# Key and value products in two parts, statistics ordered apart, and another hand-written order: a fused linear-attention and feed-forward kernel

## The chip, the cores and the metric

The kernel runs on one core of a Trainium2 chip. The metric is the device time of one execution in microseconds (us). Before the change it is 236.49 us, the median of three runs (236.43 to 236.63).

A core has five engines that run their own instruction streams and meet through semaphores: TensorE (PE in the profile, with its weight loads listed as PEld), VectorE (DVE), ScalarE (ACT), GpSimd (POOL) and SyncE (SP), which here only starts transfers. PSUM has eight banks, into which TensorE writes its products; everything else works from SBUF.

## The reference

The input is one sequence of 2048 tokens with 640 features, in bfloat16. There are 32 heads of 20 features, and a hidden layer of 1728.

```python
qkv = x_norm @ wqkv                       # x_norm: layer norm of x, without scale
pq = einsum("bhsd,hdf->bhsf", q, w_phi)   # 20x20 feature map per head; pk alike
phi_q = concat([softmax(pq), softmax(-pq)])       # phi_k alike
kv  = einsum("bhsf,bhsd->bhfd", phi_k, v)
z   = einsum("bhsf->bhf", phi_k)
o   = einsum("bhqf,bhfd->bhqd", phi_q, kv) / (phi_q . z + 1e-6)
h   = x + o @ wo
out = h + silu(layernorm(h) @ w1) @ w2
```

The attention has no mask and no product of queries with keys: all keys and values are first summed into one 40x20 matrix per head, which every query then uses.

## The kernel before

The tokens are cut into 16 tiles of 128. The feature dimension of 640 is five chunks of 128. The work of a tile is a set of small steps, each a Python function `op_xx(t)`; their names appear below as in the code.

- Layer norm 1: `st` takes the statistics of tile t (two instructions over 320 features each and one that aggregates, VectorE, lines 273 and 274); `rs` makes the reciprocal root of the variance and the bias (a power and small steps on POOL, lines 280 to 289; one small step on VectorE for a single tile, line 278); `xn` normalises (VectorE, line 297, or ScalarE, line 302, by the suffix v or a). The tile is then transposed, either on TensorE with a copy out of PSUM (`xt`, line 308, and `xc`) or by a transposing DMA (`xd`).
- Weights: the key weights are transposed on TensorE (`wt`, line 322, with the copy `wc`) and multiplied by the block-diagonal feature map (`fk`, line 337; copied to SBUF by `fc`), so that one product gives the mapped keys. The feature map's block-diagonal form is made by `mk` (a mask) and `ph` (the product of mask and map, VectorE, line 198). The query weights come by transposing DMA (`lq`) and are folded by `gk` and `gc`. Copies out of PSUM are lines 169 (VectorE) and 171 (ScalarE).
- Keys and values: `kp` is the key product of a tile and `vp` its value product, ten matmuls of 320 columns each (line 370, function `proj`: five chunks, two halves). `vc` copies the values to one of ten buffers `Vp`, whose last column is one, filled by `mo` (line 207). `ke` takes the two exponentials (ScalarE, line 395), `kr` their sums per head and the reciprocals (VectorE, lines 403 and 406), `kn` multiplies the keys by them: wholly on POOL (suffix p), wholly on VectorE (v), or three quarters (q) or one quarter (d) on POOL and the rest on VectorE (lines 414 and 418). `cc` adds the tile's keys and values into the matrices of all heads: 32 small matmuls (line 427).
- Queries: `qp`, `qs`, `qr`, `qt` are the parts of a query product (line 457) for a group of tiles, `qe` the exponentials (ScalarE, line 479). Groups of tiles are 0-1, 2-5, 6-9, 10-13, 14-15.
- Attention of a tile: `dp` is 40 small matmuls (line 504), `dw`, `dr` and `do` form the quotient on VectorE and POOL (lines 522 to 539), `td` a transposing DMA.
- Output product `op` (line 566), residual sum `oa` (VectorE, line 575), sum of squares `sq` (ScalarE, line 583), layer-norm factors `sr` (POOL, lines 588 to 598), normalisation `hn` (VectorE, line 605, or POOL and ScalarE, lines 610 and 613), transposing DMA `hd`.
- Feed-forward: `up` (lines 645 and 655) and its activation `ua` for a group and a piece of the hidden layer, `yp` and `yh` (lines 691 and 704) per tile and half, `yo` and `yz` the last sum and the store.
- Loads: `lx` (x), `lk`, `lp`, `lv`, `lo`, `l1`, `l2`, `lh` on SyncE's or ScalarE's queue; warm-up matmuls `wm` (line 268).

All orders are written by hand. The string `ORDER` holds one word per step: name, arguments, engine or split, and after `@` the PSUM banks. The loop at the end of the kernel calls the functions in that order under a manual schedule, so each engine executes its instructions in exactly the order in which the words stand; only semaphores between the engines are added. No planner or cost model moves anything afterwards. A word that stands early can hold up everything behind it on its engine if its input is late.

In the order before, the ten fills `mo` stand second; the first weight transposes are followed by the first folding products; the mask product stands right behind the first tile's statistics; the key-value sums come in five runs with tiles 9 1 0 11, then 4 5 2 3 12, 8 13 10, 6 7, and 15 14.

Of the kernel before, what the change touches and what calls it, by code (L numbers as in the profile page):

```python
# [30 lines left out]
lx.12.16.s vp.1@6 st.10 xt.2@5 vp.0@0 xc.2.a xn.9.a vc.0.a vp.2@2 st.11 lo.2.5.s xn.3.v xt.3@4 xc.3.a  # L31
rs.10.12 xn.8.a vc.2.a vc.1.a kp.2@0 ke.2 st.4 xd.9 st.5 kp.3@4 lo.0.2.s ke.3 rs.4.6 vp.3@2 xn.11.v vp.9@6
vc.9.a xn.4.a kp.9@0 ke.9 vc.3.a st.12 st.13 st.6 rs.12.14 xd.8 kr.1 kn.1.p kp.8@4 ke.8 mc.1 xn.13.a xn.12.a
xd.11 vp.11@6 vp.8@0 vc.8.a xn.5.v kr.0 kp.11@2 lq.2.s ke.11 st.7 rs.6.8 xn.6.a st.14 st.15 rs.14.16 xd.4
kr.9 vp.4@4 vc.4.a xd.5 vp.5@0 kn.0.p vc.11.a kr.2 vc.5.a kn.9.p kp.5@2 kr.11 kn.11.p gk.2@4 xn.10.a gc.2.a
xd.12 vp.12@6 vc.12.v kr.3 kn.3.p kp.4@0 xn.15.a ke.4 kp.12@4 cc.9 cc.1 kr.4 kn.4.p cc.0 xn.14.v cc.11 ke.5
kr.5 kn.2.d xd.13 ke.12 kr.12 lq.4.s xd.6 kp.6@0 lq.0.s ke.6 vp.13@2 vc.13.a kp.13@4 ke.13 vp.6@0 xd.15
xd.10 gk.4@2 vp.10@4 vc.6.a lq.3.s gk.3@0 gc.4.a gc.3.a vc.10.a kn.5.q kp.10@2 kn.12.p kr.6 xn.7.a l1.3.s
kn.6.q lq.1.s gk.1@0 gc.1.a kr.13 kn.13.p cc.4 cc.5 l1.0.s ke.10 kr.10 cc.2 cc.3 cc.12 xd.14 xd.7 kr.8
kn.8.p kn.10.d vp.15@4 vc.15.a kp.15@0 ke.15 kp.14@2 gk.0@4 gc.0.a vp.7@0 ke.14 kr.14 kn.14.p qp.0.1@4  # L40
qs.0.1 qr.0.1 kp.7@2 ke.7 l2.10.13.s kr.15 l1.2.s cc.8 vc.7.v cc.13 l2.2.4.s cc.10 qt.0.1 qp.0.0@2 qs.0.0
kn.15.p qr.0.0 qt.0.0 qe.0.1 l2.4.6.s kr.7 kn.7.v l2.6.8.s qe.0.0 vp.14@0 vc.14.a qp.0.2@6 qs.0.2 cc.6 cc.7
mt qe.0.2 cc.15 cc.14 kc km.0 lh.s qp.3.0@4 qs.3.0 qr.3.0 km.1 dp.0@0 l1.4.s close dw.0.p dr.0 qt.3.0
do.0.1.p qe.3.0 qp.2.0@6 qs.2.0 qr.2.0 qt.2.0 qe.2.0 do.0.0.p dp.1@0 dw.1.p qp.1.0@4 dr.1 do.1.0.p qs.1.0
qr.1.0 qt.1.0 qe.1.0 qp.1.1@6 td.0 do.1.1.p td.1 dp.3@0 dw.3.p dr.3 do.3.0.p qs.1.1 qr.1.1 qt.1.1 qe.1.1
qp.3.2@4 qp.1.2@5 dp.2@0 dw.2.p qs.1.2 qe.1.2 do.3.1.p td.3 qs.3.2 op.0@6 dr.2 do.2.1.p do.2.0.p qe.3.2 oa.0
dp.4@0 dw.4.p td.2 sq.0 qp.2.2@5 qs.2.2 qe.2.2 op.1@6 oa.1 sr.0 qp.2.1@4 dp.6@0 dw.6.p l1.5.s l1.1.s qs.2.1
qr.2.1 hn.0.a hd.0 sq.1 qt.2.1 sr.1 hn.1.v hd.1 qe.2.1 op.3@6 oa.3 sq.3 dp.5@0 dw.5.p op.2@4 sr.3 oa.2
hn.3.a sq.2 dr.5 do.5.0.p do.5.1.p qp.3.1@6 qs.3.1 l2.0.2.s l2.8.10.s qr.3.1 dp.9@0 dw.9.p td.5 dr.9
do.9.0.p dr.6 do.6.1.p dr.4 do.4.1.p do.4.0.p td.4 qt.3.1 qe.3.1 up.0.2@4 ua.0.2 dp.7@0 sr.2 up.0.0@6 ua.0.0  # L50
dw.7.p dr.7 up.0.3@4 ua.0.3 do.6.0.p dp.8@0 dw.8.p dr.8 hn.2.a up.0.1@6 ua.0.1 td.6 do.8.0.p op.5@4 oa.5
dp.12@0 dw.12.p dr.12 yp.1.0@6 do.7.1.p do.7.0.p sq.5 td.7 hd.3 op.4@4 oa.4 sr.5 hn.5.v hd.5 do.9.1.p sq.4
td.9 sr.4 hn.4.a dp.10@0 dw.10.p yp.1.1 yp.0.1@4 yh.0.0 hd.2 hd.4 yo.1 dp.11@0 dw.11.p dr.11 do.8.1.p
do.11.0.p td.8 yp.0.0 yo.0 op.7@6 oa.7 sq.7 dr.10 op.6@0 oa.6 sq.6 sr.6 op.9@2 up.1.6@4 do.11.1.v td.11 oa.9
sq.9 dp.15@0 ua.1.6 sr.9 up.1.5@6 ua.1.5 up.1.1@4 hn.9.v hd.9 do.10.0.p dw.15.p dr.15 hn.6.v hd.6 op.8@6
oa.8 sq.8 op.11@0 ua.1.1 sr.7 hn.7.v hd.7 up.1.3@2 oa.11 do.12.1.p sr.8 hn.8.v do.15.0.p dp.14@4 dw.14.p
dr.14 do.14.0.v hd.8 ua.1.3 up.1.4@0 ua.1.4 do.14.1.v td.14 up.1.0@2 sq.11 sr.11 hn.11.v ua.1.0 up.2.6@4
ua.2.6 dp.13@0 dw.13.p dr.13 do.13.1.p up.2.0@6 up.2.5@4 ua.2.5 op.14@0 up.1.2@2 ua.2.0 oa.14 sq.14 up.2.2@4
ua.1.2 do.12.0.p td.12 sr.14 op.12@6 oa.12 ua.2.2 hn.14.v do.10.1.p do.15.1.v yp.4.0@0 up.2.4@2 ua.2.4 td.10
op.10@4 oa.10 up.2.1@6 sq.12 sr.12 hn.12.a hd.11 hd.12 up.2.3@2 ua.2.1 yp.2.0@4 ua.2.3 yp.9.0@6 do.13.0.p  # L60
# [697 lines left out]
```

## Time and profile before

| what | value |
|---|---|
| median of three runs | 236.49 us |
| profiled execution, own time | 236.35 us |
| its span | 234.4 us |
| TensorE busy | 230.5 us, 98% of the span, 2674 matmuls |
| TensorE weight loads | 148.4 us, beside the matmuls |
| VectorE busy | 133.5 us, 249 instructions |
| ScalarE busy | 114.5 us, 171 instructions |
| POOL busy | 95.4 us, 190 instructions |
| granted TensorE clock | 1.00 in all stages |

The span is the time from the first to the last instruction in the trace; the execution is some 2 us longer, for what lies around it. Busy time is a sum over stages. The engines beside TensorE are close to full only in the first part: between 38 and 68 us VectorE is busy 28.19 of 30 us, between 160 us and the end 13.89 of 74.4.

How to read it: a row of the chain gives start, length and the work that ended last; a row of the timeline gives start, length, engine, line, output and input with their shapes, and in square brackets how long the engine had been idle and for what it waited; a row of a group gives busy time and the mean length in nanoseconds of one instruction. Consecutive chain pieces of TensorE hide short waits inside them; they show when equal pieces have unequal lengths.

### The profile page before, as it was taken

To read this page: it belongs to the slowest core of one execution; us is meant where nothing else is said; L and a number is where in the kernel's file an instruction comes from. 1 tells how busy PE (TensorE), PEld (TensorE's weight loads), DVE (VectorE), ACT (ScalarE), POOL (GpSimd) and SP (SyncE) were. 2 spreads that over 40 slices of the span, in tenths; PEclk is the share of its full clock that TensorE was granted. 3 is DMA by queue.
4 is the path that set the end of the run, shared out by engine and by line. 5 is a ranking of instruction groups with operands and counts; after the bars stand their busy time and mean duration, and the time that the engine had idled before them with its cause. 6 is when DMAs were issued, how large, how long until landed. Compare 5 with 4: busy or idle time off the path is not lost.

```text
span 234.4 us, 6307 instructions
## 1 busy us (share of the span) xinstructions
PE 230.5 (98%) x2674; PEld 148.4 (63%) x2674; DVE 133.5 (57%) x249; ACT 114.5 (49%) x171; POOL 95.4 (41%) x190
## 2 busy tenths in 40 slices
PE   8999999999999999999999999999999999999995
PEld 4777777776554556876645455556776865566662
DVE  3999999999968899788956641301341310001132
ACT  3789996885857776742244536260040015613000
POOL 7485798997904455765285123141040000000000
PEclk9999999999999999999999999999999999999999
DMA  7967758839101375325823202123212300000112
GB/s 203 381 234 147 82 112 110 182 64 350 37 3 31 59 176 148 59 49 98 142 55 61 56 3 55 30 57 63 88 24 57 106 27 5 0 3 2 54 34 81
DMA packets 44844, 20.67 MB, mean 88 GB/s; under 512 B 34448, under 2 KB 44304, under 8 KB 44816
## 3 DMA queue, kind: packets, MB, share of 16 engines
q1 hardware_dynamic: 43728, 19.88, 36.1%
q10 hardware_dynamic: 1088, 0.39, 0.8%
q8 instruction: 21, 0.34, 0.6%
q14 instruction: 7, 0.06, 0.1%
HBM read 9.61 MB, written 2.62 MB: 52 GB/s over the span
## 4 chain that ended last, share of the span: by engine, by line
PE 98%; ACT 1%; DVE 0%; issue 0%
PE mm L691 24%; PE mm L645 24%; PE mm L370 19%; PE mm L457 10%; PE mm L566 9%; PE mm L504 3%; PE mm L268 2%; PE mm L427 2%; PE mm L337 1%; PE mm L655 1%; PE mm L704 1%; ACT EqT L479 1%; PE mm L322 1%; PE mm L308 0%; DVE ob L721 0%
## 5 line engine op out<-in xcount | busy, mean ns | idle before, releaser
L691 PE MATMUL mm<-w,shT 128*128 128x320 bf16 (+2 forms) x416 | 58.7, 299 | 0.0
L645 PE MATMUL mm<-HnT,w 128*128 128x512 bf16 (+1 forms) x325 | 58.6, 337 | 0.0
L691 PEld LDWEIGHTS <-shT 128*128 128x128 bf16 x416 | 39.6, 98 | 17.2 <-issue 1.1
L667 ACT ACTIVATE shT<-mm 128x1024 bf16<-128x1024 f32 (+2 forms) x29 | 27.6, 963 | 44.6 <-PE mm L645 43.1
L712 DVE TENSOR_TENSOR ob<-mm,X 128x640 bf16<-128x640 f32 x15 | 12.3, 819 | 62.3 <-PE mm L691 59.3
L645 PEld LDWEIGHTS <-w 128*128 128x128 bf16 x325 | 31.4, 98 | 23.2
L370 PEld LDWEIGHTS <-XnT 128*128 128x128 bf16 x320 | 30.8, 98 | 12.0
L414 POOL TENSOR_TENSOR Ek<-Ek,Sk 128x1280 bf16<-128x1280 bf16 (+2 forms) x15 | 32.9, 2217 | 4.0 <-DVE Sk L406 4.0
L539 POOL TENSOR_TENSOR o<-u,rd 128x320 bf16<-128x320 f32 x28 | 19.9, 727 | 22.9 <-DVE rd L533 16.4
L583 ACT ACTIVATE sq<-X 128x640 bf16<-128x640 bf16 x16 | 11.7, 732 | 28.3 <-DVE X L575 27.2
L566 PE MATMUL mm<-wo,ot 128*128 128x320 bf16 x160 | 23.9, 299 | 0.3 <-ACT EqT L479 0.3
L457 PE MATMUL mm<-XnT,Wfq 128*128 128x512 bf16 x100 | 23.8, 380 | 0.0
L370 PE MATMUL mm<-wv,XnT 128*128 128x320 bf16 x160 | 23.7, 299 | 0.0
L370 PE MATMUL mm<-Wfk,XnT 128*128 128x320 bf16 x160 | 23.5, 299 | 0.0
L395 ACT ACTIVATE Ek<-mm 128x640 bf16<-128x640 f32 x32 | 20.5, 714 | 6.0 <-PE mm L370 5.1
L403 DVE TENSOR_REDUCE Sk<-Ek 128x64 f32<-128x1280 bf16 x16 | 23.2, 1452 | 0.3 <-ACT Ek L395 0.3
L479 ACT ACTIVATE EqT<-mm 128x1024 bf16<-128x1024 f32 (+1 forms) x24 | 19.7, 879 | 4.9 <-PE mm L457 4.8
L575 DVE SCALAR_TENSOR_TENSOR X<-mm,X 128x640 bf16<-128x640 f32 x16 | 13.0, 818 | 15.4 <-PE mm L566 15.1
L566 PEld LDWEIGHTS <-ot 128*128 128x128 bf16 x160 | 15.7, 98 | 7.3 <-issue 0.2
L273 DVE BATCH_NORM_STATS2 stats<-X 128x6 f32<-128x320 bf16 x32 | 13.6, 467 | 3.8 <-DMA X<-in_A_x_dram 3.8
L457 PEld LDWEIGHTS <-Wfq 128*128 128x128 bf16 x100 | 9.1, 98 | 9.3
L525 DVE TENSOR_TENSOR u<-mm,w 128x672 f32<-128x672 f32 x16 | 13.7, 857 | 1.2 <-DVE w L523 0.3
(78 smaller groups left out, 204.3 us busy)
## 6 DMA issues: line engine op xcount, KB each, us to landing
out_dram<-ob SPq DMA_DIRECT2D x15, 160.0 KB, 1.8
w<-in_B_w_dram SPq DMA_DIRECT2D x6, 360.0 KB, 4.5
X<-in_A_x_dram SPq DMA_DIRECT2D x3, 640.0 KB, 7.8
w<-in_B_w_dram SPq DMA_DIRECT2D x5, 320.0 KB, 5.8
wk<-in_A_wqkv_dram SPq DMA_DIRECT2D x4, 160.0 KB, 4.2
wv<-in_A_wqkv_dram SPq DMA_DIRECT2D x1, 480.0 KB, 6.4
wo<-in_A_wo_dram SPq DMA_DIRECT2D x1, 480.0 KB, 9.7
w<-in_B_w_dram SPq DMA_DIRECT2D x1, 480.0 KB, 4.6
```

Of the source, the lines that this page charges most:

```text
L370: nc.tensor.matmul(ps[:, half, 0:320], tok(XnT[t // GT], t)[:, c, :], W[:, c, half * 320 : (half + 1) * 320], start=(c == 0), stop=(c == C ...
L395: nc.scalar.activation(Ek[:, s, :].rearrange("p (a n) -> p a n", a=2), tl["kp", t][:, :, 0:320], AF.Exp, scale=1.0 - 2.0 * s,)
L403: nc.vector.tensor_reduce(Sk[:], tl["ek", t][:].rearrange("p s (h f) -> p (s h) f", f=DH), axis=AX.X, op=ALU.add,)
L414: nc.gpsimd.tensor_tensor(Ek3[:, 0:n], Ek3[:, 0:n], Sk[:, 0:n].unsqueeze(2).to_broadcast([P, n, DH]), op=ALU.mult,)
L457: nc.tensor.matmul(tl["qp", g, i][:, k, :], Wfq[:, c, r * P : (r + 1) * P], XnT[g][:, c, :], start=(c == 0), stop=(c == C - 1),)
L479: nc.scalar.activation(E[:, s, rs[0] : rs[-1] + 1, :], tl["qp", g, i][:, 0 : len(rs), :], AF.Exp, scale=1.0 - 2.0 * s,)
L525: nc.vector.tensor_tensor(u[:], A[1][:, :, :, 0:21], w[:].unsqueeze(3).to_broadcast([P, 4, 8, 21]), op=ALU.mult,)
L539: (nc.vector if eng == "v" else nc.gpsimd).tensor_tensor(tl["o", t][:, a * 320 : (a + 1) * 320].rearrange("p (h f) -> p h f", f=DH), tl["u ...
L566: nc.tensor.matmul(ps[:, half, 0:320], tl["ot", t][:, c, :], wo[:, c, half * 320 : (half + 1) * 320], start=(c == 0), stop=(c == C - 1),)
L645: nc.tensor.matmul(ps[:, i * W : (i + 1) * W], w1[:, c, fc * P : (fc + 1) * P], HnT[g][:, c, 0:W], start=(c == 0), stop=(c == C - 1), skip ...
L667: nc.scalar.activation(sh[:, a:b], tl["up", g, k][:, 0 : b - a], AF.Silu)
L691: nc.tensor.matmul(ps, shT[g][:, fc * W + i * P : fc * W + (i + 1) * P], w2[:, fc, a:b], start=first and fc == 0, stop=last and fc == FC - ...
```

## The change

1. The key product `kp` and the value product `vp` do only the first three chunks (six matmuls); new steps `kq` and `vq` do the other two (four matmuls) into the same PSUM banks. Other steps may stand between the parts.
2. The first half of a tile's statistics becomes a step of its own, `sa`; `st` does the second half and the aggregate.
3. The whole string `ORDER` is written anew from the first word to the last. Per step, the counts of copies by engine change: weight copies on ScalarE two to three of five; token copies on ScalarE three to two of four; value copies on ScalarE 14 to 15 of 16; normalisations `hn` on ScalarE six to nine of 16; attention quotients on VectorE four to eight halves of 32 in place of POOL; one `kn` that was mostly on VectorE goes to POOL whole. The numbers of matmuls, of transfers and of all steps stay.

Places in the new order that are spoken of below: the transposes `wt.1`, `wt.4`, `wt.2` and `xt.0` stand in a row ahead of the first fold `fk.0`; `ph` stands behind `st.1`; the first key product's first part stands ahead of the fold `fk.4`; the fills `mo` stand behind the power steps of tiles 2 and 3; `cc` comes in the runs 3 1 0, then 9 12 2 11, 10 7 4 6 5, and 13 8 14 15; `hn.1` is on ScalarE ahead of `qe.2.1`; the third piece of w1 (`l1.2`) stands behind `td.4` and `td.5` on SyncE's queue.

The diff, with the order cut to the lines just named:

```diff
 ORDER = """
-mk mo lx.0.1.a lk.0.1.s lp.a lx.1.2.s lk.4.5.a wm.512@7 wm.512@7 wm.512@7 wm.512@7 wm.512@7 wm.512@7
-wm.512@7 wm.512@7 wt.0@0 lk.1.2.s ta wc.0.a wm.256@2 wm.256@2 wm.256@2 wm.256@2 wm.256@2 wm.256@2 wt.1@1 wc.1.a st.0 rs.0.1
-ph.v fk.0@2 fc.0.a st.1 lk.2.3.s wt.2@4 wc.2.v lk.3.4.s wt.3@5 wc.3.v fk.1@6 fc.1.a rs.1.2 fk.2@0 fc.2.a
-lx.2.4.s xn.0.v lx.8.12.s wt.4@4 wc.4.v lv.0.3.s fk.3@2 fc.3.a xt.0@5 xn.1.v xc.0.v st.2 fk.4@6 fc.4.a
-rs.2.3 lv.3.5.s mc.0 xt.1@4 xc.1.a st.9 st.8 rs.8.10 lx.4.8.s st.3 rs.3.4 kp.0@0 ke.0 xn.2.a kp.1@2 ke.1
...
+lx.0.1.a mk sa.0 lk.0.1.s lp.a lx.1.2.s lk.4.5.a lk.1.2.s ta wm.512@7 wm.512@7 wm.512@7 wm.512@7 wm.512@7
+wm.512@7 wm.512@7 wm.512@7 wt.0@0 wc.0.a wm.256@2 wm.256@2 wm.256@2 wm.256@2 wm.256@2 wm.256@2 wt.1@1 wt.4@2
+st.0 rs.0.1 xn.0.a lk.2.3.s wt.2@3 sa.1 xt.0@4 lk.3.4.s st.1 ph.v fk.0@6 wc.4.v rs.1.2 wt.3@5 wc.1.a wc.2.a
+lx.2.4.s fk.1@0 fc.0.a xc.0.v fc.1.a fk.2@2 fc.2.a wc.3.v fk.3@4 fc.3.a xn.1.v xt.1@6 sa.2 kp.0@0 sa.3
+xc.1.v fk.4@2 st.3 kp.1@6 rs.3.4 fc.4.a kq.0 ke.0 kq.1 st.2 rs.2.3 lx.8.12.s mo lv.0.3.s xn.2.a xn.3.v sa.9
+xt.3@4 xc.3.a st.9 ke.1 sa.8 st.8 lv.3.5.s lx.4.8.s lx.12.16.s sa.11 st.11 vp.1@2 vq.1 vc.1.a sa.10 vp.0@0
+rs.8.10 lq.2.s xn.8.a kp.3@4 kq.3 xn.9.v xd.9 xt.2@6 xc.2.a vq.0 vp.3@2 vq.3 st.10 rs.10.12 ke.3 sa.4
+xn.11.a vp.2@6 vq.2 mc.0 vc.0.a vc.3.a kp.2@4 kq.2 ke.2 sa.13 sa.5 st.4 st.5 lo.0.2.s gk.2@0 vp.9@2 gc.2.a
...
+cc.3 kn.1.q cc.1 cc.0 st.14 kn.11.p sa.15 st.15 rs.14.16 ke.12 xn.14.a lq.4.s gk.4@4 gc.4.a kp.6@2 kr.9 xd.7
...
+kr.4 kn.9.p kn.2.p xd.10 cc.9 lq.1.s kn.12.p cc.12 cc.2 kr.5 kr.6 cc.11 kp.10@2 kq.10 kn.5.p kn.6.p ke.7
...
+qp.2.1@0 dp.6@2 dw.6.p hn.0.a qs.2.1 td.3 op.3@6 oa.3 do.2.1.p td.2 sq.1 sr.1 hn.1.a dr.4 do.4.0.p qr.2.1
+qt.2.1 do.4.1.p dr.6 qe.2.1 dp.5@2 l1.4.s dw.5.p dr.5 hd.0 do.6.1.p do.6.0.p qp.3.1@6 qs.3.1 qr.3.1 do.5.0.p
+op.2@0 oa.2 dp.9@2 dw.9.p dr.9 qt.3.1 qe.3.1 hd.1 up.0.2@0 ua.0.2 do.5.1.p do.9.0.p dp.7@2 dw.7.p dr.7 sq.3
+sr.3 do.9.1.v up.0.0@6 td.4 op.4@0 ua.0.0 sq.2 sr.2 hn.2.a dp.8@2 do.7.1.p oa.4 td.5 op.5@6 dw.8.p dr.8
+do.8.0.p oa.5 td.6 l1.2.s up.0.1@0 ua.0.1 sq.5 up.0.3@2 ua.0.3 do.7.0.v td.9 dp.12@4 dw.12.p do.8.1.p td.8
...
 """
+    def op_sa(t):
+        tl["stats", t] = sm.tile([P, 2, 6], F32, name="stats")
+        nc.vector.bn_stats(tl["stats", t][:, 0, :], X[:, t, 0:320])
+
     def op_st(t):
-        stats = sm.tile([P, 2, 6], F32, name="stats")
-        for k in range(2):
-            nc.vector.bn_stats(stats[:, k, :], X[:, t, k * 320 : (k + 1) * 320])
+        stats = tl["stats", t]
+        nc.vector.bn_stats(stats[:, 1, :], X[:, t, 320:D])
         nc.vector.bn_aggr(MV[:, t, :], stats[:])
...
-    def proj(t, W):
-        ps = mm2()
-        for c in range(C):
+    def proj(t, W, ps, cs):
+        for c in cs:
             for half in range(2):
                 nc.tensor.matmul(
                     ps[:, half, 0:320], tok(XnT[t // GT], t)[:, c, :], W[:, c, half * 320 : (half + 1) * 320],
                     start=(c == 0), stop=(c == C - 1),
                 )
-        return ps
 
     def op_vp(t):
-        tl["vp", t] = proj(t, wv)
+        tl["vp", t] = mm2()
+        proj(t, wv, tl["vp", t], range(3))
+
+    def op_vq(t):
+        proj(t, wv, tl["vp", t], range(3, C))
...
     def op_kp(t):
-        tl["kp", t] = proj(t, Wfk)
+        tl["kp", t] = mm2()
+        proj(t, Wfk, tl["kp", t], range(3))
+
+    def op_kq(t):
+        proj(t, Wfk, tl["kp", t], range(3, C))
```

More of the change, by code (lines that the diff above doesn't have):

```diff
@@ L31 @@
[L31 to L60, printed above, removed]
@@ new lines @@
+cc.15 qe.0.1 mt qe.0.0 qp.3.0@0 qs.3.0 qr.3.0 kc km.0 km.1 qe.0.2 dp.0@2 close dw.0.p qt.3.0 lh.s dr.0
+do.0.0.p qe.3.0 qp.2.0@6 qs.2.0 qr.2.0 qt.2.0 l2.2.4.s lo.2.5.s l2.6.8.s qe.2.0 dp.1@2 dw.1.p do.0.1.p
+qp.1.0@0 qs.1.0 dr.1 do.1.0.p qr.1.0 qt.1.0 td.0 qe.1.0 qp.1.1@6 l2.8.10.s dp.3@2 qs.1.1 qr.1.1 qt.1.1
+dw.3.p dr.3 qe.1.1 do.1.1.p qp.3.2@0 qp.1.2@1 dp.2@2 dw.2.p dr.2 qs.1.2 qe.1.2 do.3.1.p qs.3.2 qe.3.2 op.0@6
+oa.0 sq.0 do.3.0.p dp.4@2 dw.4.p do.2.0.p qp.2.2@1 qs.2.2 qe.2.2 l2.10.13.s td.1 l2.0.2.s op.1@6 sr.0 oa.1
@@ new lines @@
+op.9@0 td.7 oa.9 yp.0.1@2 hn.3.a hd.3 sr.5 hn.5.a hd.5 hd.2 dp.10@4 dw.10.p sq.4 sr.4 yh.0.0@0 yp.1.0 hn.4.a
+hd.4 yp.1.1 yo.1 sq.9 op.8@4 op.6@6 oa.8 oa.6 dr.12 do.12.0.v do.12.1.v yp.0.0 sq.6 dp.14@4 dr.10 yo.0
+up.1.2@0 ua.1.2 up.1.5@2 sr.6 ua.1.5 hn.6.v hd.6 dw.14.p dr.14 do.14.1.v dp.15@4 dw.15.p sr.9 hn.9.v dr.15
+op.7@0 oa.7 do.14.0.p td.14 do.10.0.p up.1.1@2 do.10.1.v sq.7 hd.9 sr.7 hn.7.v ua.1.1 sq.8 sr.8 hn.8.v
+up.1.4@4 ua.1.4 up.1.6@6 do.15.0.v ua.1.6 dp.13@0 up.1.3@4 td.12 op.12@6 dw.13.p dr.13 up.1.0@0 ua.1.0
@@ new lines @@
+do.15.1.p hd.7 hd.8 ua.1.3 up.2.3@2 op.14@0 ua.2.3 oa.12 sq.12 sr.12 hn.12.v td.10 op.10@6 oa.10 sq.10 sr.10
+up.2.2@4 ua.2.2 up.2.0@2 ua.2.0 up.2.6@6 ua.2.6 oa.14 dp.11@0 dw.11.p dr.11 do.11.1.v yp.4.1@4 do.13.1.p
+up.2.1@6 do.13.0.p td.13 op.13@0 ua.2.1 oa.13 up.2.4@2 ua.2.4 up.2.5@6 ua.2.5 yp.6.0@0 yp.6.1 td.15 op.15@2
+oa.15 do.11.0.p td.11 sq.13 sr.13 hd.12 hn.13.a op.11@6 oa.11 sq.11 yp.4.0 sr.11 yp.8.1@2 hd.13 hn.10.a
+sq.15 yh.2.0 yo.6 yh.1.0@6 yp.2.1 yp.8.0 yo.8 yo.4 hn.11.a yp.2.0 yo.2 yp.7.0@0 yp.5.1@2 hd.10 hd.11
@@ L68 @@
+yp.3.1@4 yh.2.1@6 yh.1.1 yp.5.0 yo.5 yp.3.0 yo.3 up.3.2@2 sr.15 hn.15.v yp.9.1 hd.15 yp.7.1 yo.7 sq.14 sr.14
+hn.14.v hd.14 up.3.4@4 ua.3.4 yp.9.0 yo.9 up.3.0@0 ua.3.0 up.4.0@4 up.3.1@6 ua.3.1 up.4.1@0 ua.4.1 ua.4.0
+up.3.5@6 up.3.3@0 ua.3.5 ua.3.3 ua.3.2 up.3.6@4 ua.3.6 yp.11.0@6 yp.10.1@0 yp.12.1@2 up.4.2@4 ua.4.2 yp.10.0
+up.4.3@4 yh.3.0 yp.12.0 yo.12 ua.4.3 yp.14.0@4 yp.15.1@2 yo.10 yh.4.0 yh.3.1@0,1 yp.15.0 yo.15 yp.14.1 yo.14
+yp.11.1 yo.11 yp.13.0 yz.13.0.s yp.13.1 yz.13.1.a
 """
```

16 lines of the change are left out of this document (9 added, 7 removed).

## The prediction

> **What bounds the kernel.** I read the page first, then what TensorE waited for, then the chain of work that ended last. Page:
>
> ```profile
> span 234.4 us, 6307 instructions
> PE 230.5 (98%) x2674; PEld 148.4 (63%) x2674; DVE 133.5 (57%) x249; ACT 114.5 (49%) x171; POOL 95.4 (41%) x190
> PEclk9999999999999999999999999999999999999999
> ```
>
> TensorE is busy 98% of the span, at its full granted clock in every slice. The change keeps the 2674 matmuls, so only idle TensorE time can move the end. TensorE's listed waits, and the chain (start, length, what), show how little there is:
>
> ```profile
> PE mm L268 <- PEq L742: 0.8, 1, 0.8
> PE mm L566 <- ACT EqT L479: 0.3, 1, 0.3
> ```
>
> ```profile
> 6.25 0.45 PE mm L322 x5
> ...
> 7.58 0.80 PE mm L337 x12
> ...
> 8.65 0.32 PE mm L337 x6
> 8.96 0.28 PE mm L308 x5
> 9.24 0.48 PE mm L337 x6
> 9.72 0.32 PE mm L308 x5
> 10.04 4.19 PE mm L370 x30
> ...
> 34.13 4.07 PE mm L370 x30
> 38.20 1.32 PE mm L427 x128
> ...
> 48.73 1.54 PE mm L427 x160
> ...
> 65.20 1.13 PE mm L427 x128
> ...
> 77.47 0.40 PE mm L504 x40
> ...
> 79.27 1.36 PE mm L566 x10
> ...
> 84.43 1.85 PE mm L457 x8
> 86.30 1.95 ACT EqT L479 x2
> ```
>
> The first 0.8 us is the start, which both kernels have. The rest hides inside chain pieces that are longer than equal pieces elsewhere. Early: 12 matmuls of line 337 take 0.80 where twice the undisturbed 0.32 would do (0.16 lost), six take 0.48 (0.16), five transposes 0.32 instead of 0.28 (0.04), and the first 30 of line 370 take 4.19 instead of 4.07 (0.12): 0.48 us. In the key-value product (line 427): 128 matmuls take 1.32 and 1.13, and 160 take 1.54 where 160/128 of 1.13 is 1.41: 0.19 + 0.13 = 0.32 us. Before the tenth output product (line 566): 0.3 us. Together 1.1 us, 0.5% of the span, is the most that a reordering could win; what it can lose has no such bound.
>
> **The change, part by part.**
>
> *Splitting the key and value products* adds no instruction: three plus two of the five contraction chunks make the same ten matmuls. A piece of the product can now start before the last weight chunk is there, and another piece of work can stand between the parts. The switch costs nothing that the chain shows: line 370 runs at 0.136 us a matmul (4.07/30) beside transposes. Taken at 0; bounds ±0.1 over all, since the row 10.04 shows 0.12 in 30 matmuls.
>
> *Splitting the statistics* (first half, then second half with the aggregate) is the same instruction count on VectorE. It lets the mask product (line 198) go after the first two tiles' statistics instead of between the first tile's and its power step. That matters for the small power step on POOL; timeline rows:
>
> ```profile
> 5.08 0.99 DVE L198 TENSOR_TENSOR phb<-phr,mask 128x800 bf16<-128x800 bf16 x1
> 5.24 1.24 POOL L281 TENSOR_TENSOR RS<-RS,nhalf 128x1 f32<-128x1 f32 x1 [0.75 <-DVE RS L278]
> 6.58 0.26 POOL L283 TENSOR_SCALAR RS<-MV,RS 128x1 f32<-128x1 f32 x1
> 11.07 0.88 DVE L273 BATCH_NORM_STATS2 stats<-X 128x6 f32<-128x320 bf16 x2
> 11.24 0.55 POOL L281 TENSOR_TENSOR RS<-RS,nhalf 128x1 f32<-128x1 f32 x1 [1.66 <-DVE RS L278]
> ```
>
> The same step takes 1.24 us beside the mask product, which reads two tensors, and 0.55 beside statistics, which read one. After the change the first one runs beside statistics: 0.7 us earlier for the first normalised tile. The Trainium skill ("SBUF — State Buffer", section "Who interferes with whom") says that a VectorE instruction with two SBUF inputs and a GpSimd instruction that reads SBUF take a shared pair of ports in turn, while a reduction never contends; by that rule the step would be free of the wait, and these two rows agree.
>
> *The early order.* Durations per copy and normalisation, from the groups of instructions:
>
> ```profile
> L171 ACT COPY wTk<-mm 128x640 bf16<-128x640 bf16 x2 | 1.4, 692 | 2.3 <-PE mm L322 2.3
> L169 DVE COPY wTk<-mm 128x640 bf16<-128x640 bf16 x3 | 1.4, 487 | 0.3 <-PE mm L322 0.2
> L302 ACT ACTIVATE xn<-X,RS 128x640 bf16<-128x640 bf16 x10 | 9.2, 938 | 0.0
> ```
>
> The first tile's normalisation goes to ScalarE, and three of the five weight copies too; three groups of weight transposes and the first token transpose now stand ahead of the first folding product (line 337). I walk it with the rows. TensorE: from 6.25, where it has waited for weights that are loaded in both kernels alike, 0.45 + 0.28 + 0.28 to 7.26. The first tile's power step starts at 5.24 as before, takes 0.55 + 0.26 with the hand-over near 0.1, so 6.15; the normalisation (0.94) ends at 7.1, and with two hand-overs of some 0.05 to 0.1 the token transpose waits 0 to 0.05. Then 0.28, a folding product (0.32), a transpose (0.28), two folding products: 8.8. The fourth folding product needs the copy of the transpose that ended at 8.15; VectorE takes it after the token copy, 8.3 to 8.8, and so TensorE waits about 0.1. The second token transpose waits for a normalisation on VectorE behind that, up to 0.1. So the first key product starts near 9.55, without the fifth folding product, which followed before: 10.04 - 0.32 = 9.72. A gain of 0.17, and its third chunk then waits some 0.1 for a folded weight, against the 0.12 of before. Taken 0.15; bounds 0 (ScalarE, with a longer piece and three longer copies, falls behind by what it saves) and 0.3.
>
> *The key-value product.* Its waits are for POOL's normalised keys. Groups:
>
> ```profile
> L414 POOL TENSOR_TENSOR Ek<-Ek,Sk 128x1280 bf16<-128x1280 bf16 x11 | 26.9, 2456 | 4.0 <-DVE Sk L406 4.0
> L414 POOL TENSOR_TENSOR Ek<-Ek,Sk 128x960 bf16<-128x960 bf16 x2 | 3.9, 1942 | 0.0
> L418 DVE TENSOR_TENSOR Ek<-Ek,Sk 128x960 bf16<-128x960 bf16 x2 | 2.4, 1212 | 0.0
> ```
>
> The first group before took tiles 9, 1, 0 and 11, four whole tiles on POOL (4 x 2.46 = 9.8 us), and the wait of 0.19 stood ahead of it. The first group after has tiles 3, 1 and 0 only, and of tile 1 a quarter goes to VectorE, so POOL owes it 2 x 2.46 + 1.94 = 6.9 us; later groups stand further behind their keys in the new order. Over all tiles, one of which three quarters lay on VectorE (1.21) goes back to POOL whole. VectorE, with 28.2 of 30 us busy in this stage (next row), so gets 1.2 us of room, and POOL, with 23.9, has it. I take both waits as gone, a gain of 0.3 (bounds 0 and 0.32). Next in line is the last key tile, whole on VectorE, with the last group waiting on it; by the walk it is some 0.3 us early, and if POOL took 10% longer a tile (2.7) over the three tiles before it, 3 x 0.25 less 0.3, some 0.4, would come back.
>
> ```profile
> 38.00:68.00 30.00, 30.00 (x706) 20.64 (x708) 28.19 (x32) 22.24 (x38) 23.93 (x13) 1.00 0.59 134
> ```
>
> (Window, PE, PEld, DVE, ACT, POOL busy, clock, DMA.)
>
> *More copies on ScalarE.* One value copy and three hidden-layer normalisations go from VectorE to ScalarE, four attention products back from POOL to VectorE. Over the span ScalarE gains some 3 us on 114.5 and VectorE changes by less: none of these engines is the bound, their work lies beside TensorE's, and POOL gets lighter; so 0, except at one place. Normalising tile 1 (0.92 us, second row below) now sits on ScalarE ahead of the exponentials of query part 2.1, which the third output product needs. For tile 0 the whole chain (residual sum to the end of the normalisation) is on the timeline:
>
> ```profile
> 80.74 0.83 DVE L575 SCALAR_TENSOR_TENSOR X<-mm,X 128x640 bf16<-128x640 f32 x1
> 84.35 0.92 ACT L613 ACTIVATE hn<-X,hm 128x640 bf16<-128x640 bf16 x1 [0.89 <-POOL hm L610]
> ```
>
> From 80.74 to 85.27 that is 4.5 us; with the two exponentials (1.95 in the chain) 6.5 us. TensorE's cover between the second output product and the one that waits is 17 query matmuls at 0.216 (line 457: 8 in 1.85 is 0.231 with an edge), one output product (1.36) and two of line 504 (0.40 each): 5.8 us. A wait of 0.65 at most; tile 0's chain held 0.2 to 0.4 of waits for another, so 0.3 is likelier, as long as the wait of before. Taken: no gain, no loss; bounds -0.3 and +0.35.
>
> *Transfers.* The order on SyncE's queue changes; of the moves, the one with least room is that the third piece of w1 is now issued after two attention transposes, by my walk near 94.4, and wanted near 99.8. Rows:
>
> ```profile
> w<-in_B_w_dram SPq DMA_DIRECT2D x6, 360.0 KB, 4.5
> w<-in_B_w_dram SPq DMA_DIRECT2D x5, 320.0 KB, 5.8
> ```
>
> The first group is w1's pieces, the second w2's. At 4.5 it lands 0.9 before need; at the 5.8 that the second group shows, though smaller, it would be 0.4 late. Taken 0, bound +0.4. Later pieces of w2 go earlier than their use by many us, so 0.
>
> *The ten small fills of the value tiles* (line 207) leave POOL's start, where they cost nothing, for about 13 us, ahead of the power steps of tiles 8 and 9. Rows, timeline and groups:
>
> ```profile
> 13.79 0.24 POOL L280 TENSOR_SCALAR RS<-MV 128x2 f32<-128x2 f32 x1
> 15.20 0.19 POOL L289 TENSOR_SCALAR RS<-RS 128x2 f32<-128x2 f32 x1
> L207 POOL MEMSET Vp<- 128x32 bf16 x10 | 1.5, 481 | 0.0
> ```
>
> Ten took 1.5 us together. The power steps of a pair of tiles take 1.6 (13.79 to 15.39). From 13.0, when the power step of tile 2 is done: 14.5, 16.1, ready for the normalisation of tile 8 on ScalarE. That engine is by my walk with the value copy of tile 1 until about 16.6; then 0.94 and the copy of tile 2 behind it (0.69): near 18.2. TensorE wants that copy for its value product of tile 2, after the first key product's six matmuls (0.82), the fifth fold (0.32), two groups of transposes (0.56) and 54 matmuls at 0.136 (7.34): 9.55 + 9.04 = 18.6. With 0.5 to spare on ScalarE and 0.4 on TensorE, the slack is 0.9, so the cost is 0; the price without that cover is rival (c).
>
> **Sum.** 0.15 + 0.3 = 0.45 us gained, less 0.05 for the new tight places: 0.4. The profiled execution took 236.35 us, 0.14 under the median; 236.49 - 0.4 = 236.1.
>
> **Rivals.** The measurement tells apart 0.2%, 0.47 us: "faster" is under 236.02.
>
> (a) The savings do not appear: the early waits and those for the keys come back elsewhere, for the engines beside TensorE are 90% busy there (28.2 of 30 us) and any wait removed exposes the next. 236.3 to 236.7. Against it: the first group asks for one tile fewer.
>
> (b) Normalisation on ScalarE or w1's third piece sets the pace: 0.35 + 0.4 at their bounds, less part of the gain, +0.5: 237.0. It decides from 0.45 us on. For it: cover 5.8 against a chain of 6.5. Against: part of that chain was waits.
>
> (c) The other side: the fills at 13 us. Each record lasts 0.48 us, and ten overlapped to 1.5 at a time when VectorE had nothing to do; if beside VectorE's statistics they stand in line, ten take 4.8 us, 3.3 more. The slack of 0.9 leaves 2.4 us of stall, less the 0.4: 238.5. It decides when the ten take over 2.4 us. Against it: the power step kept its 0.55 us beside statistics, and a fill reads nothing.
>
> (d) The keys are late for the last group, by POOL running 10% to 20% slower beside more VectorE work with two inputs: 0.35 to 0.7 and no gain in that product: 237.1.
>
> (e) The clock. The early order puts twenty transposes in a row after the warm-up. If these let the granted clock fall to half over work of 3.75 us, the next row's length, and if half of that work falls into it, 1.9 us are added, less the 0.4: 238.0. Against: before ran thirty transposes among 61 matmuls in this row at a granted 1.00.
>
> ```profile
> 6.25:10.00 3.75, 3.75 (x61) 3.25 (x61) 3.44 (x11) 3.26 (x6) 1.59 (x4) 1.00 1.01 364
> ```
>
> The Trainium skill ("TensorE: Matmul & The Clock Gate", Part 4, on the transpose) says that transposes on TensorE do not count as busy and the clock does not rise for them; the row disagrees at least for this mixture, so I keep it small.
>
> **How the numbers follow.** Main case 0.55 (235.7 to 236.3; likeliest 236.1), (a) 0.16, (b) 0.11, (c) 0.09, (d) 0.07, (e) 0.02. Of the main case somewhat over half lies under 236.02, its middle being just there: faster 0.31. Within 0.2%: the rest of it and nearly all of (a), 0.40. Slower: 0.29. The range 235.7 to 237.2 leaves out (c), (e) and small tails, under 0.2.
>
> **What would show it.** Right: the third and sixth line-337 rows near 0.32 for six; the 128 and 160 matmuls of line 427's successor (438) at 1.13 and 1.41; the first power step at 0.55; a wait of about 0.3 for the exponentials; the ten fills in 1.5 us. Wrong: a new waiter beside the third output product or for w1; the fills spread out; the last key-value group waiting on VectorE; a granted clock below 1.00 early.

## The result and the profile after

The changed kernel takes 237.09 us (median of ten runs, 236.71 to 237.57), the kernel before on the same occasions 236.42 us (236.13 to 236.63). The ratio is 1.0027, 95% interval 1.0018 to 1.0035: 0.6 us slower, a small loss that is clear of the measurement. The forecast was 236.1, 0.4 us shorter than before. The profiled execution of the changed kernel took 236.73 us, with a span of 234.8 against 234.4; it is one of the faster ones, so the traces show 0.4 of the 0.6 us.

The page of the changed kernel:

```profile
span 234.8 us, 6308 instructions
PE 230.2 (98%) x2674; PEld 148.0 (63%) x2674; DVE 131.7 (56%) x248; ACT 116.8 (50%) x175; POOL 95.1 (40%) x189
PEclk9999999999999999999999999999999999999999
PE 84%; DVE 7%; ACT 3%; POOL 2%; DMA 1%; issue 1%; DVEq 0%; POOLq 0%
```

TensorE has the same work and the same clock. But the chain that ended last, 98% TensorE before (its summary line was `PE 98%; ACT 1%; DVE 0%; issue 0%`), is now TensorE for 84%: in places other engines lead. What TensorE waited for (total, times, longest):

```profile
PE mm L270 <- PEq L753: 0.8, 1, 0.8
PE mm L313 <- ACT xn L307: 0.4, 1, 0.4
PE mm L577 <- ACT EqT L490: 0.3, 1, 0.3
PE mm L438 <- DVE maskS L226: 0.2, 1, 0.2
```

Two waits are new in this list: one ahead of the first token transpose (line 313) and one in the key-value sums (line 438). The chain and TensorE's timeline of the changed kernel around the places that the prediction named:

```profile
9.74 0.93 PE mm L374 x6
...
45.60 1.18 PE mm L438 x128
...
66.48 1.62 PE mm L468 x7
...
92.80 2.19 PE mm L656 x20
...
232.06 0.29 DVE ob L732
```

```profile
64.92 0.66 PE L438 MATMUL mm<-Ek,Vp 128*21 128x40 bf16 x64
65.83 0.66 PE L438 MATMUL mm<-Ek,Vp 128*21 128x40 bf16 x64 [0.25 <-DVE maskS L226]
```

Some points of the run are reached with exactly the same TensorE work behind them in both kernels, so their times can be compared directly. The start of the last 128 sums is read from the timeline in both kernels, because the chain of the changed kernel has no row there; the other points are from the chains. For before, the prediction shows 10.04 and 65.20 + 1.13 = 66.33, and these are its further rows, the first from the timeline:

```profile
65.13 1.20 PE L427 MATMUL mm<-Ek,Vp 128*21 128x40 bf16 x128
```

```profile
92.47 2.18 PE mm L645 x20
...
231.67 0.29 DVE ob L721
```

| point | before | after | after less before |
|---|---|---|---|
| first key product starts, with five folds done (after: 9.74 and the fifth fold's 0.32) | 10.04 | 10.06 | 0.0 |
| last 128 matmuls of the key-value sum start | 65.13 | 64.92 | -0.2 |
| they are done | 66.33 | 66.48 | +0.15 |
| first hidden piece starts | 92.47 | 92.80 | +0.35 |
| last output sum starts | 231.67 | 232.06 | +0.4 |

So in this pair of executions the early part won nothing, the removed waits of the key-value sums won 0.2 of the forecast 0.3, the last group of these sums lost 0.35 again, and 0.2 more went between there and the first hidden piece. After that 140 us pass with hardly a difference. The experiments look at these places one by one.

### The profile page after: what moved, and what is told of

The parts are those of the page before. It is cut to its first block, busy times and chain, and to the rows that moved or that the text cites. A ratio compares the mean times of both kernels' runs of the same rounds, so it can differ in the third digit from the quotient of the medians.

```text
span 234.8 us, 6308 instructions
## 1 busy us (share of the span) xinstructions
PE 230.2 (98%) x2674; PEld 148.0 (63%) x2674; DVE 131.7 (56%) x248; ACT 116.8 (50%) x175; POOL 95.1 (40%) x189
## 4 chain that ended last, share of the span: by engine, by line
PE 84%; DVE 7%; ACT 3%; POOL 2%; DMA 1%; issue 1%; DVEq 0%; POOLq 0%
PE mm L656 24%; PE mm L702 24%; PE mm L374 16%; PE mm L577 8%; PE mm L468 5%; DVE Sk L414 3%; PE mm L515 2%; PE mm L342 1%; DVE Ek L429 1%; DMA X<-in_A_x_dram 1%; PE mm L666 1%; PE mm L438 1%; PE mm L715 1%; DVE Sk L417 1%; ACT EqT L490 1%
## 5 line engine op out<-in xcount | busy, mean ns | idle before, releaser
L425 POOL TENSOR_TENSOR Ek<-Ek,Sk 128x1280 bf16<-128x1280 bf16 (+2 forms) x15 | 33.8, 2278 | 3.4 <-DVE Sk L417 3.4
L550 POOL TENSOR_TENSOR o<-u,rd 128x320 bf16<-128x320 f32 x24 | 17.9, 762 | 21.5 <-DVE rd L544 15.8
L374 PE MATMUL mm<-Wfk,XnT 128*128 128x320 bf16 x160 | 24.2, 299 | 0.0
L539 DVE TENSOR_TENSOR u<-u,mm 128x672 f32<-128x672 f32 x16 | 13.7, 853 | 0.6
```

The lines of the kernel that those rows point to most:

```text
L374: nc.tensor.matmul(ps[:, half, 0:320], tok(XnT[t // GT], t)[:, c, :], W[:, c, half * 320 : (half + 1) * 320], start=(c == 0), stop=(c == C ...
L425: nc.gpsimd.tensor_tensor(Ek3[:, 0:n], Ek3[:, 0:n], Sk[:, 0:n].unsqueeze(2).to_broadcast([P, n, DH]), op=ALU.mult,)
L550: (nc.vector if eng == "v" else nc.gpsimd).tensor_tensor(tl["o", t][:, a * 320 : (a + 1) * 320].rearrange("p (h f) -> p h f", f=DH), tl["u ...
```

## Experiments: is it the split or the order, and how steady is it

**The order of before under the new functions.** Every `kp` and `vp` is followed at once by its second part, every `st` is preceded by its `sa`:

```diff
-... st.0 rs.0.1 ... kp.0@0 ke.0 xn.2.a kp.1@2 ke.1 ... vp.1@6 st.10 ...
+... sa.0 st.0 rs.0.1 ... kp.0@0 kq.0 ke.0 xn.2.a kp.1@2 kq.1 ke.1 ... vp.1@6 vq.1 sa.10 st.10 ...
```

> The two-part products and statistics of the changed kernel, but in the order of the kernel before, each second part right behind its first. If the order makes the loss (T1, T2): ratio to before 1.000 within 0.1%, 236.2 to 236.7 us. If the split functions themselves cost (T3: 32 more places where matmuls change over): 0.1% to 0.3% slower, 236.7 to 237.2.

Measured: 236.37 us, ratio 0.9993 (0.9983 to 1.0004). In the order of before, the split costs nothing that these runs can tell; the loss comes with the new order.

**The changed kernel again**, twice, with other profiles.

> The changed kernel once more, for a second profile and as the base of the other three. All theories: 0.2% to 0.35% slower than before (236.9 to 237.4 us). The profile of the first execution (236.73, the second fastest of ten) cannot tell what the usual 237.1 has on top. Theory T2 (a transposing transfer of an attention tile is held up by the w2 pieces issued around it): where this execution takes 237.0 or more, TensorE waits 0.2 to 0.5 us ahead of the second output product (line 577, near 82 us), which had 0.6 us to spare in the first profile. Theory T1 (fixed order only): the same waits as in the first profile, 0.4 ahead of the first token transpose, 0.25 to 0.42 ahead of the last key-value groups, 0.3 to 0.45 ahead of the third output product, and no other.

> The changed kernel a third time, as the base of the next three on one chip. All theories: 0.1% to 0.3% slower than before.

Measured: 236.98 us, ratio 1.0016 (1.0007 to 1.0024), a little less than expected, and 237.03 us, ratio 1.0025 (1.0015 to 1.0036). The profiles took 236.80 and 236.81 us. They show the waits of the first profile (the second has one for the key weights in place of the one for the first normalised tile) and none ahead of the second output product. No profile is of an execution of over 237.0, so that part of the expectation stays untested.

**The w2 loads earlier.** In the changed kernel's trace one attention transpose was issued at 76.26 between w2 pieces and took 5.2 us instead of 2.6.

```diff
-... l2.6.8.s qe.2.0 ... td.0 qe.1.0 qp.1.1@6 l2.8.10.s ... l2.10.13.s td.1 l2.0.2.s op.1@6 ...
+... l2.6.8.s l2.8.10.s l2.10.13.s l2.0.2.s qe.2.0 ... td.0 qe.1.0 qp.1.1@6 ... td.1 op.1@6 ...
```

> The changed kernel with the three last w2 pieces issued before the first attention transpose instead of between the first and the fourth. T2: the transpose issued at 76.3 lands in 2.6 instead of 5.2 us, the kernel is 0.2 to 0.4 us shorter than the changed one (236.7 to 236.9) and varies less from run to run (0.9 us between the extremes of ten before this). T1: no change within 0.1 us, the transfer has 0.6 us to spare.

Measured: 236.79 us, ratio 1.0015 (1.0004 to 1.0025), between 236.60 and 237.60. Not to be told apart from the changed kernel (1.0016 beside it on the same chip), and no steadier. The late transfer is not the cause of the loss.

What does move from execution to execution is the start. Here are three profiles of kernels with the new early order, each with the first load of x and the start of the first key product. Of the six profiles in which the chain starts with this load, they are the one with the shortest load (the kernel with the mask made twice, below), that of the changed kernel (its second row stands above), and the one with the longest load (a kernel with one normalisation moved, below):

```profile
0.79 3.04 DMA X<-in_A_x_dram
...
9.62 0.94 PE mm L374 x6
```

```profile
0.79 3.16 DMA X<-in_A_x_dram
```

```profile
0.79 3.27 DMA X<-in_A_x_dram
...
9.84 0.94 PE mm L374 x6
```

The first load ends 0.12 and 0.11 us later, and the first key product starts 0.12 and 0.10 later. In these executions the first load's time passes to TensorE one to one. In others, as in the second repeat of the changed kernel, the chain starts with the key weights instead (first key product at 9.56). That profile still took 236.81 us, so the start alone does not tell how long an execution is.

## Experiments: the mask in POOL's queue

The second half of the mask `mc.1` is two small POOL instructions (lines 216 and 220). The change had moved it from early in the run to between the last key normalisations: the diff in the first part cuts that line out, and it reads `cc.10 kn.7.p cc.7 kr.8 kn.8.q cc.4 cc.6 cc.5 mc.1 ke.13 ... kn.13.p ... kn.14.d`. POOL and VectorE in the timeline of the changed kernel:

```profile
59.84 0.38 POOL L216 TENSOR_SCALAR_AFFINE_SELECT maskR<-maskR 128x192 bf16<-128x192 bf16 x1
60.19 1.09 DVE L429 TENSOR_TENSOR Ek<-Ek,Sk 128x960 bf16<-128x960 bf16 x1
60.28 1.24 POOL L220 TENSOR_SCALAR_AFFINE_SELECT maskR<-maskR 128x192 bf16<-128x192 bf16 x1
...
61.49 4.28 POOL L425 TENSOR_TENSOR Ek<-Ek,Sk 128x1280 bf16<-128x1280 bf16 x2
...
63.40 1.79 DVE L429 TENSOR_TENSOR Ek<-Ek,Sk 128x1280 bf16<-128x1280 bf16 x1
...
65.11 0.66 DVE L226 STREAM_TRANSPOSE maskS<-maskR 128x480 bf16<-128x480 bf16 x1
```

The last row is what the list of waits names, but the key-value sums do not use the transposed mask. POOL's two normalisations (tile 13, and a quarter of tile 14) end at 61.49 + 4.28 = 65.77, and so does VectorE's transpose (65.11 + 0.66). TensorE starts 0.06 later at 65.83. The place of the wait says which of them it is: the 64 matmuls before it are tiles 13 and 8, the next is tile 14, and of tile 14 VectorE's part was done at 60.19 + 1.09 = 61.28 and POOL's at 65.77. The list took the one engine for the other. Two experiments test whether the mask in POOL's queue is what made POOL late.

**Mask early:**

```diff
-st.6 rs.6.8 lq.3.s gk.3@6 ...
+st.6 rs.6.8 mc.1 lq.3.s gk.3@6 ...
...
-... cc.4 cc.6 cc.5 mc.1 ke.13 ...
+... cc.4 cc.6 cc.5 ke.13 ...
```

> The changed kernel with the second half of the mask (mc.1, two POOL instructions, 0.4 and 1.24 us in the profile) moved from between the last normalised keys to about 30 us earlier. T1, with the wait ahead of the last key-value groups as its largest new term: the quarter of tile 14 on POOL ends 1.2 us or more sooner, the wait at 65.4 us goes, 0.3 to 0.42 us shorter than the changed kernel: 236.6 to 236.8. If POOL would be held up there anyway by the ports it shares with VectorE's normalisations: 0 to 0.1 shorter.

> mask_early a second time, beside the changed kernel and the two others. 0.25 to 0.45 us shorter than the changed kernel if the masks' place is the cause; equal to it within 0.15 if the first result was chance.

Measured: 236.54 us, ratio 0.9999 (0.9991 to 1.0007), and the second time 236.66, ratio 1.0011 (1.0002 to 1.0020); the changed kernel beside them 1.0016 and 1.0025. That is 0.4 us shorter both times (236.98 - 236.54, 237.03 - 236.66). The traces show about half of that, for the profiled executions of the changed kernel were shorter than its median: the key-value sums are done at 66.24 in place of 66.48. Rows of the first, POOL's, VectorE's for tile 15, and TensorE's:

```profile
25.77 0.38 POOL L220 TENSOR_SCALAR_AFFINE_SELECT maskR<-maskR 128x192 bf16<-128x192 bf16 x1
...
60.50 5.03 POOL L425 TENSOR_TENSOR Ek<-Ek,Sk 128x1280 bf16<-128x1280 bf16 x2 [0.56 <-DVE Sk L417]
...
63.45 1.49 DVE L429 TENSOR_TENSOR Ek<-Ek,Sk 128x1280 bf16<-128x1280 bf16 x1
...
64.97 1.26 PE L438 MATMUL mm<-Ek,Vp 128*21 128x40 bf16 x128
```

The select takes 0.38 at its early place against 1.24 beside VectorE's three-quarter normalisation of tile 14. The 128 matmuls run in one piece of 1.26 where they took 65.83 + 0.66 - 64.92 = 1.57. POOL's two tiles end at 65.53 instead of 65.77, although they start 1.0 us earlier: now they overlap VectorE's two-input instruction and take 5.03 instead of 4.28. The Trainium skill ("SBUF — State Buffer", "Who interferes with whom") states the rule behind it, that a GpSimd instruction which reads SBUF and a VectorE instruction with two SBUF inputs exclude one another, the first to issue holding the shared ports for its whole length. The 0.38 and 1.24 of the same select agree, and so does the 0.75 that passes on to the next one.

**Mask made twice**, in its late place:

```diff
-... cc.4 cc.6 cc.5 mc.1 ke.13 ...
+... cc.4 cc.6 cc.5 mc.1 mc.1 ke.13 ...
```

> The changed kernel with the second half of the mask made twice in its place (the two selects repeat, with the same result). If POOL is what the last key-value groups wait for, every added microsecond there comes out at the end: 0.8 (two selects at 0.38 to 0.40) to 1.2 us slower than the changed kernel, 237.8 to 238.2, and the wait near 65.4 grows from 0.42 to 1.2 to 1.6. If the groups wait for VectorE's whole tile 15 (as the profile's line says, it names VectorE): no more than 0.1 slower.

Measured: 237.70 us (four runs, 237.68 to 237.72), ratio 1.0055 (1.0040 to 1.0071). The changed kernel did not run beside it; against the ratios that it had on other occasions (1.0016 to 1.0027) this is 0.7 to 0.9 us more, the lower edge of what was expected. Its timeline:

```profile
62.02 0.38 POOL L220 TENSOR_SCALAR_AFFINE_SELECT maskR<-maskR 128x192 bf16<-128x192 bf16 x1
...
62.37 4.29 POOL L425 TENSOR_TENSOR Ek<-Ek,Sk 128x1280 bf16<-128x1280 bf16 x2
63.39 2.69 DVE L429 TENSOR_TENSOR Ek<-Ek,Sk 128x1280 bf16<-128x1280 bf16 x1
...
66.71 0.47 PE L438 MATMUL mm<-Ek,Vp 128*21 128x40 bf16 x42 [1.14 <-DVE maskS L226]
```

POOL ends 0.89 later (66.66 against 65.77), TensorE goes on 0.88 later (66.71 against 65.83). POOL's queue sets the end of the key-value sums, and here the two added selects (0.76 us) count in full.

The path does not stay on POOL, though. With POOL's two instructions read one by one, the three versions show the same chain:

| | changed | mask early | mask twice |
|---|---|---|---|
| POOL's tile 13 starts | 61.49 | 60.50 | 62.37 |
| it ends | 63.84 | 63.55 | 64.73 |
| VectorE's tile 15 ends (lines above) | 65.19 | 64.94 | 66.08 |
| POOL's quarter of tile 14 ends | 65.77 | 65.53 | 66.66 |

VectorE's tile 15 starts at 63.4 in all three, but it lasts 1.49 to 2.69 us and always ends 1.35 to 1.39 after POOL's tile 13. POOL's quarter takes 1.97 to 2.02 us, where one of the two in the kernel before took 0.72, and always ends 0.58 or 0.59 after VectorE's tile 15. So each engine held the other up. It also explains why 1.0 us of earlier start gave only 0.24 at the end: with the mask early, POOL's tile 13 took 3.05 instead of 2.35 us, because it met VectorE's part of tile 14 (60.25 to 61.34). And VectorE's transpose of the mask, next behind tile 15, ends with POOL's quarter in all three (65.53 and 66.67 in the other two), which is why the list names it.

## Experiments: the normalisation ahead of the exponentials

The output product that waits for the exponentials is that of tile 2, called the third above, though it is the fourth to run (0, 1, 3, 2). In the changed kernel the chain runs through the normalisation of tile 1 on ScalarE into the exponentials:

```profile
86.38 0.56 POOL hm L609
...
87.34 0.68 ACT hn L624
...
88.17 1.92 ACT EqT L490 x2
...
90.13 1.52 PE mm L577 x10
91.65 0.40 PE mm L515 x40
92.05 0.75 PE mm L468 x3
92.80 0.22 PE mm L656 x2
```

**Tile 1 on VectorE**, with the mask early and, in another kernel, with the mask left late:

```diff
-... sq.1 sr.1 hn.1.a dr.4 ...
+... sq.1 sr.1 hn.1.v dr.4 ...
```

> mask_early with the normalisation of hidden tile 1 back on VectorE, where before had it. If ScalarE's normalisation ahead of the exponentials is what lengthened the wait of the third output product (0.34 before, 0.43 after): the wait falls to 0.2 or less and the kernel is 0.2 to 0.4 us shorter than mask_early, 236.15 to 236.35. If VectorE is as full there as ScalarE: the wait is shorter but one on VectorE takes its place at the first hidden piece (near 91.7): within 0.1 us.

> The changed kernel with only the normalisation of hidden tile 1 back on VectorE, the mask left where the change put it. If the two losses are separate (the masks' place at 65 us, ScalarE's order at 88 us): 0.25 to 0.35 us shorter than the changed kernel, with the wait of 0.42 at 65.4 us still there and the one ahead of the third output product at 0.2 or less. If the second was only ever the tail of the first: no change.

Measured: with the mask early 236.17 us, ratio 0.9995 (0.9986 to 1.0004), which is 0.1 to 0.4 us under the two ratios of the mask early (0.9999 and 1.0011, from other occasions); alone 236.68, ratio 1.0014 (1.0005 to 1.0023), 0.35 us under the changed kernel beside it. The chain of the first:

```profile
88.32 1.24 PE mm L468 x5
89.56 0.01 issue
89.57 1.52 PE mm L577 x10
91.09 0.40 PE mm L515 x40
91.49 0.16 issue
91.65 0.59 PE mm L468 x2
92.24 0.77 PE mm L656 x7
```

The exponentials and the normalisation are gone from the chain, TensorE leads it again, and the list of waits no longer names the output product. From the end of the key-value sums to the first hidden piece it takes 92.24 - 66.18 = 26.06 us (the sums are a row of 1.20 us from 64.98 in its chain), with tile 1 on ScalarE 92.80 - 66.48 = 26.32, in the kernel before 92.47 - 66.33 = 26.14. So the trace shows 0.26 us at this place. In the trace of the other kernel, with the mask late, it is 92.87 - 66.70 = 26.17, so 0.15; there the wait of the key-value sums is still listed and the one ahead of the output product is gone, as expected.

**Query matmuls first**, over the mask early: three matmuls of the next query product go ahead of the product that waits.

```diff
-... qp.3.1@6 qs.3.1 qr.3.1 do.5.0.p op.2@0 oa.2 dp.9@2 dw.9.p dr.9 qt.3.1 qe.3.1 ...
+... qp.3.1@6 qs.3.1 qr.3.1 qt.3.1 do.5.0.p op.2@0 oa.2 dp.9@2 dw.9.p dr.9 qe.3.1 ...
```

> mask_early with the last three query matmuls (0.65 us of TensorE work) moved ahead of the third output product. If that product only lacks cover while the exponentials are made: its wait of 0.43 goes, 0.3 to 0.4 us shorter than mask_early, 236.1 to 236.25. If the wait is a chain on one pair of PSUM banks (exponentials read it, output product fills it, residual sum reads it, first hidden piece fills it): the wait turns up at the hidden piece near 91.5, with 0.3 to 0.65 us, and the total is the same to 0.25 us longer.

Measured: 236.65 us, ratio 1.0015 (1.0006 to 1.0023): not shorter than with the mask early alone (0.9999 and 1.0011); whether it is longer, these runs can't tell. The wait of 0.27 ahead of the output product is gone, and it moved as the second reading had it:

```profile
92.81 1.36 PE L656 MATMUL mm<-HnT,w 128*128 128x256 bf16 x11 [0.60 <-DVE X L586]
```

The exponentials, the output product, the residual sum and the hidden piece pass one pair of PSUM banks (0 and 1) on to each other, by the banks that the order names. Here more cover ahead of one link made the next one wait; an earlier start of the chain, which the normalisation on ScalarE had put off, shortened it.

## Experiments: the early order, and all together

**The early order of before**, over the mask early. The words ahead of the ten fills stand nearly as in before:

```diff
-... wt.0@0 wc.0.a ... wt.1@1 wt.4@2 st.0 rs.0.1 xn.0.a ... wt.2@3 sa.1 xt.0@4 ... st.1 ph.v fk.0@6 ... xt.1@6 ... kp.0@0 ... xc.1.v fk.4@2 ... kp.1@6 ... kq.0 ... kq.1
+... wt.0@0 ... wc.0.a ... wt.1@1 wc.1.a sa.0 st.0 rs.0.1 ph.v fk.0@2 fc.0.a sa.1 st.1 ... xn.0.v ... fk.4@6 fc.4.a xt.1@4 xc.1.a kp.0@0 ... kq.0 ... kp.1@6 kq.1
```

> mask_early, with the words up to the ten fills put back into the sequence of the kernel before (mask product behind the first statistics, first tile normalised on VectorE, weight transposes between the folds; the first key product behind the fifth fold again). If the new early order saved the forecast 0.15 us and something later hid it: 0.1 to 0.2 us slower than mask_early, 236.65 to 236.75. If both early orders come out at the same time, bound by the chain from the first load of x to the folded weights on ScalarE (the rows of TensorE's lateness say so: equal at 20 us): within 0.1 us of mask_early, 236.45 to 236.65.

Measured: 236.48 us, ratio 1.0007 (0.9998 to 1.0016), between the two results of the mask early (0.9999 and 1.0011). No difference that these runs can tell. The trace has the first key product with five folds at

```profile
10.15 0.94 PE mm L374 x6
```

and two more profiles with the old early order have 10.04 and 10.12. The eleven profiles with the new one have it at 9.56 to 9.84 and the fifth fold's 0.32: 9.88 to 10.16, on the mean 10.01. So the new order gains some 0.1 us there, up to 0.2 in some executions and nothing in others.

**Mask early, tile 1 on VectorE and w2 earlier** together:

> Mask early, hidden tile 1 on VectorE and the w2 pieces ahead of the attention transposes together. If the losses add: 0.55 to 0.75 us shorter than the changed kernel and 0.1% faster than before or more (236.0 to 236.2). If only the larger of them counts: as mask_early.

Measured: 236.43 us, ratio 1.0005 (0.9996 to 1.0013), 0.6 us under the changed kernel beside it (237.03). The two losses add in the main: 0.4 for the mask and 0.35 for the normalisation alone, 0.6 together here, and 0.5 to 0.7 in the kernel with both but without the loads (1.0016 or 1.0025 less 0.9995). The expected 0.1% under before did not come: no version was found that is clearly faster than before.

The chain of this run has one more loss, inside the first attention product (40 matmuls of line 515):

```profile
67.79 0.19 PE mm L515 x7
67.98 0.45 issue
68.43 0.40 PE mm L515 x33
```

These 40 matmuls take 0.42 us in both profiles with the order of before, 0.48 to 0.67 in eleven with the new order, and 1.04 here. In the gap neither TensorE nor its weight loads work, and the profile shows nothing that they wait for; the cause is open. Of the 0.2 us that the changed kernel lost between the sums and the first hidden piece, 0.07 is at this product (0.49 against 0.42).

## Why the prediction was wrong

The forecast was 0.4 us shorter, and the kernel is 0.6 us longer: 237.09 us, inside the stated range of 235.7 to 237.2, but on the other side of before.

- *The bound.* Right: TensorE's idle time is all that moved, and the clock stayed at full rate, also over the twenty transposes in a row (5.86 to 7.74), so rival (e) fell.
- *The split functions.* Right: 0, by the order of before under them.
- *The key-value product.* Most of the forecast gain came: the last run of the sums starts 0.2 earlier, not 0.3, and the runs ahead of it kept a little of their waits (128 matmuls take 1.18 in the row at 45.60 above, where 1.13 would do). The step that failed is the sentence "Next in line is the last key tile, whole on VectorE", with the 0.3 us by which it was to be early. TensorE waited 0.25 us for the tile before it, whose quarter on POOL ended at 65.77. Two things were missing. The working left out an instruction group that the change moves into POOL's queue: the second half of the mask, which costs 0.4 us in the times and 0.24 in the traces. And it walked POOL and VectorE side by side at uniform mean prices, where the runs show POOL's tile 13, VectorE's tile 15 and POOL's quarter of tile 14 one behind the other. The profile's own pair of power steps (1.24 against 0.55), which the same text quotes for the early part, said what a two-input VectorE instruction does to POOL. Rival (d) had the place, a fair price and, in VectorE's work with two inputs, part of the mechanism; it did not have the mask, and its chance was too small (0.07).
- *Normalising tile 1 on ScalarE.* Mis-sized. It was taken at no loss, because the wait of before (0.3) would be of the same length. So it was (0.27 in both traces), but the new order without this edit would hardly have the wait and is 0.35 us shorter: against that, the edit costs what the upper bound allowed (+0.35). Rival (b) had this half of its mechanism right; its other half, the load, did not come. The prediction's "tenth output product" is the same product, the fourth to run.
- *The early order.* Forecast 0.15; in the first pair of traces 0.0, on the mean of all profiles 0.1 (10.10 against 10.01), and no difference in the times. The first pair is partly chance: the first load of x ended at 0.79 + 3.16 = 3.95 in the changed kernel's execution, and VectorE began on it at 3.83 in that of before. In the six profiles in which the new order starts with this load, the first key product follows its end by 5.78 or 5.79 us. The step that the walk had wrong is the wait for the first normalised tile, taken at 0 to 0.05: it was up to 0.6, where the key weights landed early or the first load late. The loads of these weights are issued alike in both kernels (1.70 to 1.74), but the second group of transposes starts anywhere from 5.35 to 6.40 in the new order's profiles. Where it started at 6.14, in the second repeat, that wait is absent and the first key product starts at 9.56, the walk's 9.55.
- *The fills.* Right, rival (c) fell: ten took 1.51 us beside VectorE's statistics. They had taken 1.51 in before too, from 2.97 to 4.48, and there VectorE was idle only up to 3.83, not all the time as the prediction says.

```profile
13.38 1.51 POOL L209 MEMSET Vp<- 128x32 bf16 x10
```

- *Transfers.* Right: the third piece of w1 brought no wait. It was issued at 95.37 (94.4 by the walk), landed 3.5 later, and the matmuls that read it started at 100.80. Moving w2 pieces changed nothing in the times.

In all, by the table of points: 0 early, 0.2 gained by 65 us, 0.35 lost in the last key-value run, 0.2 up to the first hidden piece, 0.05 after: 0.4 us, which is the profiled execution. The usual execution is 0.2 longer than that against before; what makes this 0.2 is open. The start, which follows the first load or the weights, and the first attention product both vary by as much between profiles, but no profile fell on an execution of that length. With both losses undone the kernel is equal to before within 0.1% (0.9995 and 1.0005, with intervals of 0.1% to each side). In its trace 0.2 us of the 0.45 forecast as gains is left at the first hidden piece (92.24 against 92.47); the times can't confirm even that.
